# Eight PSUM-to-SBUF adds of one batch moved from VectorE to ScalarE copies and GpSimd adds, and one scalar load moved behind the first keys

## The chip, the cores and the metric

The kernel runs on one core of one Trainium2 chip. The time is the device time of one execution, in microseconds (us); times are compared as medians of several executions. The engines are named as in the profile: PE (TensorE; PEld is its weight load), DVE (VectorE), ACT (ScalarE), POOL (GpSimd) and SP (SyncE, which only issues transfers here). Each engine works through its own instructions in the order in which the program lists them.

## The reference: what is computed

Thresholded attention, then one block of an MLP mixer, all in float32. Batch 8, 8 heads, 576 tokens, 64 columns per head, so 512 columns per token.

```
scores = q @ k.T / 8
scores = where(scores >= max(scores) - tau, scores, -1e9)
attn   = exp(scores - max(scores)); attn /= sum(attn) + 1e-9
x      = (attn @ v), heads side by side         # (8, 576, 512)
h      = relu(x.T @ w_tok1) @ w_tok2            # over tokens: 576 -> 256 -> 576
u      = x + h.T
out    = u + relu(u @ w_ch1) @ w_ch2            # over columns: 512 -> 1536 -> 512
```

## The kernel before, in words

The work goes in *units* of 128 query tokens for one pair of heads: 18 units for each batch, 144 in all. Unit u runs `scores(u)` (L304 matmuls into PSUM, L309 row maximum on DVE, L310 bias on POOL), `weigh(u)` (ACT: L319 `e`, which thresholds, and L326, the exponential with its row sum), and one unit later `norm` (L333 and L334 on DVE, L337 on POOL). Two units later the weights `e` are turned: in batch 0 by PE (L355) and copies (L357), from batch 1 on by DVE's block transposes (L367) and sixteen transfers issued by SP (L376). `values` multiplies them with v (L411, L416), which leaves x, transposed, in the tile `xT` (by L423 on DVE in batch 0, L421 on ACT after that).

The MLP of one batch is a list of steps with costs, laid between the units of the next batch: `fill(share)`, called at several places of each unit, takes steps from the deque `todo` until a quota of cost is used up. `token_mlp(b)` gives the steps `turn_x` (PE transposes L447, copied to `x_sb` by ACT, L448), `tok1` (L454, relu to `a` by ACT L456) and `tok2` (L464: one product of 128 columns by 288 tokens into PSUM; L468: DVE adds it to `xT` in place). `channel_mlp` gives `ch1` (L507, relu to `g` by ACT L508) and `ch2` (L528). Batch 0 is special: its first two column blocks are started early, in `early`, and its last two when `push(0)` is called after its last unit. All eight `tok2` steps of batch 0 run in units 19 to 22, when the products have their own PSUM pool `ps_mm` with two buffers, shared with `ch1` and `ch2`. Until then and for some 30 us after, the weights still arrive: int64 words from memory are turned into float32 by a chain over SP (L178 load), ACT (L193, L195), DVE (L203, L205, L209) and POOL (L217, an add of two SBUF operands), one *piece* after the other, paced by `weight(2)` three times per unit.

At the start, tau is loaded by ACT's queue (L89), then the first queries by SP and the first keys by ACT, four transfers each (L105); DVE computes three small columns from tau (L265 to L269: `tlow`, `toff`, `ntau`) and then transposes queries and keys (L286). `toff` is read first by POOL's bias, `ntau` by ACT's exponential. Every transfer signals one of eight semaphores in turn, and a transfer that gets a semaphore already in use first waits for the earlier one to land.

The lines that matter:

```
439:    return (ps_mm or ps_tr).tile([P, DM], F32, tag="mm" if ps_mm else "tr", name=name)
467:    u = xT[:, c, o + HS * f : o + HS * f + HS]
468:    nc.vector.tensor_add(out=u, in0=u, in1=to)
474:    steps += [(0.97, lambda c=c, f=f: tok2(c, f)) for c in ps for f in range(2)]
```

Of the kernel before, what the change touches and what calls it, by code (L numbers as in the profile page):

```python
# [9 lines left out]
F32 = mybir.dt.float32  # L10
# [4 lines left out]
ALU = mybir.AluOpType  # L15
AX = mybir.AxisListType

P = 128
# [3 lines left out]
def kernel(  # L22
# [25 lines left out]
    nc = tc.nc  # L48
# [12 lines left out]
    NCC = DM // P  # L61
    NJ = DCH // P
    HS = S // 2
    NK = 2 * S // P
    GR = 2 * P
    SCALE = 1.0 / 8.0
# [3 lines left out]
    work = ctx.enter_context(tc.tile_pool(name="work", bufs=2))  # L70
# [7 lines left out]
    ps_mm = None  # L78
# [7 lines left out]
    UB = 9 * NP // 2  # L86

    tau_sb = const.tile([P, 1], F32, name="tau_sb")
    nc.scalar.dma_start(out=tau_sb, in_=bass.AP(tensor=tau.tensor, offset=0, ap=[[0, P], [1, 1]]))  # L89


    loaded = {}
# [3 lines left out]
    def load_qk(n, eng, parts=range(8)):  # L96


        b, p = pairs[n]
        if n not in loaded:  # L100
            loaded[n] = [ld.tile([P, S // 32, 32], F32, tag=tag, bufs=1, name=f"{tag}_{n}") for tag in ("lq", "lk")]
        for part in parts:
            i, which = divmod(part, 2)
            h, c = divmod(i, 2)
            eng[which].dma_start(  # L105
                out=loaded[n][which][32 * i : 32 * i + 32],
                in_=(q, k)[which][b, 2 * p + h, :, 32 * c : 32 * c + 32].rearrange("(n t) d -> t n d", t=32),
            )
# [11 lines left out]
    for t in vlast:  # L120
        nc.gpsimd.memset(t, 0.0)
    load_qk(0, (nc.sync, nc.scalar))

    w1 = const.tile([P, NT, DTOK], F32, name="w1")
    w2 = const.tile([P, NTK, S], F32, name="w2")
# [117 lines left out]
    def need(i):  # L243

        weight(3 * i + 4 - steps_done)
# [14 lines left out]
    FAR = 104.0  # L260
    STEEP = 3.0e38
    tlow = const.tile([P, 1], F32, name="tlow")
    toff = const.tile([P, 1], F32, name="toff")
    ntau = const.tile([P, 1], F32, name="ntau")
    nc.vector.tensor_scalar(out=tlow, in0=tau_sb, scalar1=0.0, scalar2=-3.0e38, op0=ALU.is_lt, op1=ALU.mult)  # L265
    nc.vector.tensor_scalar(out=toff, in0=tau_sb, scalar1=0.0, scalar2=FAR, op0=ALU.max, op1=ALU.min)
    nc.vector.tensor_scalar(out=toff, in0=toff, scalar1=-1.0 / SCALE, scalar2=None, op0=ALU.mult)
    nc.vector.tensor_add(out=toff, in0=toff, in1=tlow)
    nc.vector.tensor_scalar(out=ntau, in0=toff, scalar1=SCALE, scalar2=None, op0=ALU.mult)  # L269


    heads = {}
# [8 lines left out]
    def prep(n):  # L281
        lq, lk = loaded.pop(n)
        made = []
        for src, name in ((lq, "qT"), (lk, "kT")):
            sb = work.tile([P, S], F32, tag=name, name=f"{name}_{n}")
            nc.vector.transpose(out=sb, in_=src.rearrange("p n d -> p (n d)"))  # L286
            made.append(sb)
        heads[n] = made
# [135 lines left out]


    hidden = {}

    def token_mlp(b, ps=range(NP)):

        xT = xTs[b]  # L430
        o = S * (b % 2)
        L = len(ps)
        cols = slice(P * ps[0], P * ps[0] + P * L)
        if b not in hidden:
            hidden[b] = work.tile([P, NTK, DM], F32, tag="a", bufs=1, name=f"a_{b}")
        a = hidden[b]

        def psum(name):
            return (ps_mm or ps_tr).tile([P, DM], F32, tag="mm" if ps_mm else "tr", name=name)

        def turn_x(t, n):
            M = MT[t]
            to = ps_tr.tile([P, MAIN], F32, tag="tr", name=f"tx_{b}_{t}_{ps[0]}")[0:M, 0 : n * L * P].rearrange("p (t c x) -> p t c x", t=n, c=L)
            for i in range(n):
                for c in range(L):
                    tok = o + (t + i) * P
                    nc.tensor.transpose(out=to[:, i, c, :], in_=xT[:, ps[c], tok : tok + M], identity=ident)  # L447
            nc.scalar.copy(out=x_sb[0:M, t : t + n, cols], in_=to.rearrange("q t p d -> q t (p d)"))  # L448

        def tok1(m):  # L450
            need(2)
            to = psum(f"t1_{b}_{m}_{ps[0]}")[:, 0 : P * L]
            for t in range(NT):
                nc.tensor.matmul(to, lhsT=w1[:, t, P * m : P * m + P], rhs=x_sb[:, t, cols], start=(t == 0), stop=(t == NT - 1))  # L454
            if ps_mm:
                nc.scalar.activation(out=a[:, m, cols], in_=to, func=AF.Relu)  # L456
            else:
                copies.append(lambda: nc.vector.tensor_scalar(out=a[:, m, cols], in0=to, scalar1=0.0, scalar2=None, op0=ALU.max))

        def tok2(c, f):  # L460
            need(6)
            to = psum(f"t2_{b}_{c}_{f}")[:, 0:HS]
            for m in range(NTK):
                nc.tensor.matmul(  # L464
                    to, lhsT=a[:, m, P * c : P * c + P], rhs=w2[:, m, HS * f : HS * f + HS], start=(m == 0), stop=(m == NTK - 1)
                )
            u = xT[:, c, o + HS * f : o + HS * f + HS]
            nc.vector.tensor_add(out=u, in0=u, in1=to)  # L468

        n = NI // L  # L470
        steps = [(0.11 * n * L, lambda t=t: turn_x(t, n)) for t in range(0, NI, n)] + [(0.11 * L, lambda: turn_x(NI, 1))]
        first = len(steps)
        steps += [(1.1 * L, lambda m=m: tok1(m)) for m in range(NTK)]
        steps += [(0.97, lambda c=c, f=f: tok2(c, f)) for c in ps for f in range(2)]
        return steps, (first, first + NTK)


# [101 lines left out]
    def push(b):  # L579
        nonlocal quota  # L580
        uT = xTs[b]
        steps, waits = token_mlp(b) if b else token_mlp(b, range(NP // 2, NP))
        old = list(todo)
        todo.clear()
        todo.extend(early)
        early.clear()

        for i, step in enumerate(steps):
            n = 2 if i in waits else 1
            todo.extend(old[:n] + [step])  # L590
            del old[:n]
        todo.extend(old)
        for i in range(2) if b % 2 == 0 else range(2, (2 * S + GR - 1) // GR):
            todo.extend(channel_mlp(b - b % 2, uT, i))
        quota = (sum(c for c, _ in todo) - (KEEP if b else KEEP_FIRST)) / (UB - 1)

    prep(0)
    due = deque()
    b_now = 0
    LAG = 2  # L600
# [13 lines left out]
    for u in range(len(units) + LAG + 4):  # L614
        on = u < len(units)
        if u == UB:
            late.close()
            ps_mm = ctx.enter_context(tc.tile_pool(name="ps_mm", bufs=2, space=bass.MemoryType.PSUM))
        if on:
            b_now, p0, t = units[u]  # L620
            n = b_now * NP + p0
# [24 lines left out]
        if last and u < UB:  # L646
            early.extend(token_mlp(0, range(NP // 2))[0])
        elif last:
            push(0)
# [79 lines left out]
```

## Time and profile before

| | us |
|---|---|
| median of 5 executions | 1358.22 |
| lowest, highest | 1352.83, 1359.95 |
| the profiled execution | 1359.95 |
| its span, first to last instruction | 1358.2 |
| busy in the span: PE | 1311.8 (97%) |
| DVE | 593.3 (44%) |
| ACT | 585.9 (43%) |
| POOL | 355.5 (26%) |
| mean granted PE clock | 0.992 |
| the eight adds of L468 in batch 0 | 441 to 455 ns each, from 112.5 to 144.7 us |

A profile is one execution seen by the hardware profiler. Its span is cut into 40 equal slices, with the busy share of each engine as a digit (tenths, 9 is 90% or more) and the clock that PE was granted. The *chain of waits* is followed back from the last instruction: at each step to what released it. Groups and timelines name an instruction by line, engine and operation, then `output<-inputs`; in square brackets stands how long the engine was idle before it, and what ended that. Two engines that meet in a tile wait for each other through semaphores.

### The profile page before, as it was taken

How to read it: one execution, taken by the hardware profiler on the slowest of the kernel's cores; microseconds unless marked ns; L12 is line 12 of the kernel's file. 1: busy time of each engine (PE TensorE's matmuls, PEld its weight loads, DVE VectorE, ACT ScalarE, POOL GpSimd, SP SyncE). 2: the span in 40 equal slices, each digit the busy share in tenths (PEclk: the TensorE clock that was granted, in tenths of full speed). 3: DMA queues.
4: the chain of work that ended last, by engine and by line, in shares of the span. 5: the costliest groups of instructions: out<-in, count | busy, mean ns of one | idle time of the engine just before them, and what ended most of it. 6: DMA issues, size and time to landing. Idle time of an engine off the chain costs nothing.

```text
span 1358.2 us, 17794 instructions
## 1 busy us (share of the span) xinstructions
PE 1311.8 (97%) x6138; PEld 811.6 (60%) x6138; DVE 593.3 (44%) x1024; ACT 585.9 (43%) x1299; POOL 355.5 (26%) x683
## 2 busy tenths in 40 slices
PE   6888899999999999999999999999999999999998
PEld 4555655547575566565656566465656476575675
DVE  5888874435443444534344444435443454201000
ACT  5776654445454444443435444344434453120110
POOL 4665653223222222212122222212221222100000
PEclk9998899999999999999999999999999999999999
DMA  5434764545454444443445435534443453400000
GB/s 122 105 92 126 203 154 102 122 104 118 100 125 100 95 112 109 116 109 86 96 99 125 104 77 119 135 81 106 115 103 82 111 120 76 112 24 17 23 24 32
DMA packets 296538, 135.31 MB, mean 100 GB/s; under 512 B 204736, under 2 KB 289216, under 8 KB 296448
## 3 DMA queue, kind: packets, MB, share of 16 engines
q1 hardware_dynamic: 167840, 118.15, 34.2%
q10 hardware_dynamic: 128608, 16.01, 7.4%
q8 instruction: 49, 0.80, 0.3%
q14 instruction: 41, 0.34, 0.1%
HBM read 43.25 MB, written 9.44 MB: 39 GB/s over the span
## 4 chain that ended last, share of the span: by engine, by line
PE 85%; DVE 6%; DMA 3%; ACT 3%; issue 1%; POOL 1%; SPq 0%; ACTq 0%; DVEq 0%; POOLq 0%
PE c L528 27%; PE c L507 26%; PE sc L304 11%; PE pv L416 9%; PE t L454 5%; PE t L464 4%; PE pv L411 3%; DVE mx L309 2%; ACT e L319 1%; PE tr L355 1%; PE tx L447 1%; DMA lq<-in_q_dram 1%; DMA lk<-in_k_dram 1%; ACT e L326 1%; DVE wc L205 1%
## 5 line engine op out<-in xcount | busy, mean ns | idle before, releaser
L309 DVE TENSOR_REDUCE mx<-sc 128x1 f32<-128x576 f32 x288 | 204.3, 750 | 451.8 <-PE sc L304 451.7
L507 PE MATMUL c<-xT,wc 128*128 128x256 f32 (+1 forms) x1920 | 401.3, 363 | 0.2 <-ACT g L508 0.2
L528 PE MATMUL c<-wc,g 128*128 128x512 f32 x864 | 389.5, 597 | 0.0
L507 PEld LDWEIGHTS c<-xT,wc 128*128 128x128 f32 x1920 | 335.0, 191 | 70.2 <-issue 30.1
L310 POOL TENSOR_SCALAR bias<-mx,toff 128x1 f32<-128x1 f32 x288 | 83.2, 289 | 781.8 <-DVE mx L309 725.4
L319 ACT ACTIVATE e<-sc,bias 128x576 f32<-128x576 f32 x288 | 199.6, 740 | 179.7 <-POOL bias L310 175.5
L528 PEld LDWEIGHTS c<-wc,g 128*128 128x128 f32 x864 | 158.9, 190 | 181.6 <-issue 178.2
L326 ACT ACTIVATE e<-e,ntau 128x576 f32<-128x576 f32 x288 | 221.0, 771 | 0.0
L337 POOL TENSOR_SCALAR e<-e,rr 128x576 f32<-128x576 f32 x288 | 215.1, 759 | 14.0 <-ACT g L508 2.6
L508 ACT ACTIVATE g<-c 128x256 f32<-128x256 f32 (+1 forms) x240 | 86.9, 362 | 297.2 <-PE c L507 279.1
L304 PE MATMUL sc<-kT,qT 64*128 64x288 f32 (+1 forms) x1280 | 195.5, 440 | 12.3 <-DVE kT L286 7.3
L367 DVE STREAM_TRANSPOSE T<-e 128x1152 f32<-128x1152 f32 x126 | 172.0, 1365 | 5.5 <-DMA eT<-T 3.3
L304 PEld LDWEIGHTS sc<-kT,qT 64*128 64x128 f32 (+1 forms) x1280 | 107.4, 181 | 100.6 <-issue 57.3
L416 PE MATMUL pv<-eT,lv 128*64 128x384 f32 (+1 forms) x1024 | 138.3, 411 | 0.0
L416 PEld LDWEIGHTS pv<-eT,lv 128*64 128x64 f32 x1024 | 77.0, 139 | 50.0 <-issue 41.3
L421 ACT COPY xT<-pv 128x384 f32<-128x384 f32 (+1 forms) x56 | 21.0, 400 | 167.8 <-PE pv L416 161.8
L540 DVE TENSOR_TENSOR us<-c,ut 128x512 f32<-128x512 f32 x27 | 18.6, 691 | 155.0 <-PE c L528 142.1
L464 PE MATMUL t<-w,a 128*128 128x288 f32 x256 | 76.0, 424 | 8.1 <-DVE xT L468 4.7
L454 PE MATMUL t<-x_sb,w 128*128 128x512 f32 (+1 forms) x180 | 72.6, 550 | 0.0
L464 PEld LDWEIGHTS t<-w,a 128*128 128x128 f32 x256 | 46.1, 193 | 30.3 <-issue 10.5
L468 DVE TENSOR_TENSOR xT<-xT,t 128x288 f32<-128x288 f32 x64 | 28.3, 446 | 71.0 <-PE t L464 70.5
L326 ACT ACTIVATION_READ_ACCUMULATOR e<-e,ntau 128x1 f32 x288 | 56.5, 196 | 0.0
(46 smaller groups left out, 545.7 us busy)
## 6 DMA issues: line engine op xcount, KB each, us to landing
eT<-T SPq DMA_DIRECT2D x672, 108.0 KB, 2.3
scratch<-in_moe_w_ch_dram SPq DMA_DIRECT2D x24, 512.0 KB, 3.6
lv<-in_v_dram SPq DMA_DIRECT2D x32, 288.0 KB, 3.3
out_dram<-us SPq DMA_DIRECT2D x36, 256.0 KB, 2.2
lk<-in_k_dram ACTq DMA_DIRECT2D x111, 72.0 KB, 2.8
lq<-in_q_dram ACTq DMA_DIRECT2D x106, 72.0 KB, 2.3
ut<-us SPq DMA_DIRECT2D x192, 32.0 KB, 1.9
lq<-in_q_dram SPq DMA_DIRECT2D x22, 72.0 KB, 3.2
```

The lines of the kernel that those rows point to most:

```text
L304: nc.tensor.matmul(sc[h][rows, f, 0:HS], lhsT=qT[r, cols], rhs=kT[r, HS * f : HS * f + HS], start=True, stop=True)
L309: nc.vector.tensor_reduce(out=mx[:, c], in_=sc[h][:, :, 0:HS], axis=AX.XY, op=ALU.max)
L319: nc.scalar.activation(out=eh, in_=sc[h][:, :, 0:HS], func=AF.Prelu, bias=bias[:, h : h + 1], scale=SCALE, alpha=STEEP)
L326: nc.scalar.activation(out=eh, in_=eh, func=AF.Exp, bias=ntau, accum_out=rs[:, h : h + 1])
L337: nc.gpsimd.tensor_scalar(out=eh, in0=eh, scalar1=rr[:, h : h + 1], scalar2=1.0, op0=ALU.mult, op1=ALU.mult)
L367: nc.vector.transpose(out=T[:, :, place, :].rearrange("p a (c x) -> p c a x", c=NK), in_=e.rearrange("p (c a x) -> p c a x", c=NK, a=4))
L416: nc.tensor.matmul(to[r], lhsT=lv[:, j, :], rhs=e[j], start=False, stop=(c == NI - 1), skip_group_check=True)
L454: nc.tensor.matmul(to, lhsT=w1[:, t, P * m : P * m + P], rhs=x_sb[:, t, cols], start=(t == 0), stop=(t == NT - 1))
L464: nc.tensor.matmul(to, lhsT=a[:, m, P * c : P * c + P], rhs=w2[:, m, HS * f : HS * f + HS], start=(m == 0), stop=(m == NTK - 1))
L507: nc.tensor.matmul(ps, lhsT=wc1[:, j, c, :], rhs=uT[:, c, GR * i : GR * i + n], start=(c == 0), stop=(c == NCC - 1))
L508: nc.scalar.activation(out=s["g"][:, j, 0:n], in_=ps, func=AF.Relu)
L528: nc.tensor.matmul(flat, lhsT=s["g"][:, j, P * t : P * t + P], rhs=wc2[:, j, :], start=(j == 0 and b > 0), stop=(j == NJ - 1), skip_group_ ...
```

## The change

- The eight `tok2` products of batch 0 are no longer added to `xT` by DVE from PSUM. ACT copies the product to one third of a scratch tile `h` in SBUF (the thirds are used in turn; `h` lies in the buffer `ut`, which is first needed with batch 2), and POOL adds `h` to `xT`. All other batches keep DVE's add.
- For batch 0, the `tok2` steps run all first halves of the tokens, then all second halves, instead of both halves of one column block after the other.
- The five operations on tau are the same as before, moved. The load of tau stands behind the four key transfers on ACT's queue instead of ahead of them, and DVE's five operations on tau stand behind the transposes of the first queries and keys. Tau's transfer now takes the semaphore of the first key transfer, and waits for that one; the fourth key transfer no longer waits for tau.

```diff
     tau_sb = const.tile([P, 1], F32, name="tau_sb")
-    nc.scalar.dma_start(out=tau_sb, in_=bass.AP(tensor=tau.tensor, offset=0, ap=[[0, P], [1, 1]]))
...
     load_qk(0, (nc.sync, nc.scalar))
+    nc.scalar.dma_start(out=tau_sb, in_=bass.AP(tensor=tau.tensor, offset=0, ap=[[0, P], [1, 1]]))
...
+    stage = []
+    turns = [0]
...
             u = xT[:, c, o + HS * f : o + HS * f + HS]
-            nc.vector.tensor_add(out=u, in0=u, in1=to)
+            if b == 0 and ps_mm:
+                h = work.tile([P, GR // P, 4, NCC * 32], F32, tag="ut", bufs=1, name=f"h_{c}_{f}") if not stage else stage[0]
+                if not stage:
+                    stage.append(h)
+                h = h.rearrange("q n a x -> q (n a x)")[:, HS * (turns[0] % 3) : HS * (turns[0] % 3) + HS]
+                turns[0] += 1
+                nc.scalar.copy(out=h, in_=to)
+                nc.gpsimd.tensor_tensor(out=u, in0=u, in1=h, op=ALU.add)
+            else:
+                nc.vector.tensor_add(out=u, in0=u, in1=to)
...
-        steps += [(0.97, lambda c=c, f=f: tok2(c, f)) for c in ps for f in range(2)]
+        order = [(c, f) for c in ps for f in range(2)]
+        if b == 0:
+            order.sort(key=lambda x: x[1])
+        steps += [(0.97, lambda c=c, f=f: tok2(c, f)) for c, f in order]
...
     prep(0)
+    nc.vector.tensor_scalar(out=tlow, in0=tau_sb, scalar1=0.0, scalar2=-3.0e38, op0=ALU.is_lt, op1=ALU.mult)
+    nc.vector.tensor_scalar(out=toff, in0=tau_sb, scalar1=0.0, scalar2=FAR, op0=ALU.max, op1=ALU.min)
+    nc.vector.tensor_scalar(out=toff, in0=toff, scalar1=-1.0 / SCALE, scalar2=None, op0=ALU.mult)
+    nc.vector.tensor_add(out=toff, in0=toff, in1=tlow)
+    nc.vector.tensor_scalar(out=ntau, in0=toff, scalar1=SCALE, scalar2=None, op0=ALU.mult)
```

More of the change, by code (lines that the diff above doesn't have):

```diff
@@ L264 @@
     ntau = const.tile([P, 1], F32, name="ntau")
[L265 to L269, printed above, removed]
     heads = {}
```

## The prediction

> **What bounds the kernel now.** I read the slices over the span first, then the busy time by stage, then the chain of work inside the stage that the change touches.
>
> ```profile
> PE   6888899999999999999999999999999999999998
> DVE  5888874435443444534344444435443454201000
> PEclk9998899999999999999999999999999999999999
> ```
>
> TensorE (PE) is full from the sixth slice (34 us each) to the end; VectorE (DVE) is nearly full in slices two to five only, and there alone the clock row falls to 8. By stage (core time of the stage, then PE, PEld, DVE, ACT, POOL busy, clock):
>
> ```profile
> 100.00:180.00 80.00, 71.62 (x319) 47.34 (x317) 68.77 (x113) 53.85 (x112) 48.84 (x58) 0.89 0.60 160
> 300.00:600.00 300.00, 296.44 (x1464) 183.73 (x1464) 135.09 (x228) 137.02 (x309) 77.88 (x166) 1.00 0.46 106
> ```
>
> From 300 us on PE idles 3.6 us in 300, and the change leaves PE's later work as it is. A gain or loss is thus a shift of the moment, near 180 us, at which PE becomes the bound; all of the change but the tau load lies before it. The eight adds of L468 that change run from 112.5 to 144.7 us. The chain of waits there, merged (start, us, what):
>
> ```profile
> 124.90 0.04 DVE xT L468
> 124.94 0.34 issue
> 125.28 1.37 DVE T L367
> ...
> 138.91 1.33 DVE mx L309 x2
> ...
> 141.23 0.45 DVE xT L468
> 141.69 0.04 issue
> 141.73 2.29 PE t L464 x4
> 144.02 3.41 PE c L507 x8
> 147.43 1.49 PE sc L304 x8
> ```
>
> The chain is VectorE's own order nearly throughout; the adds stand in it, and the last second product (L464) waits 2.9 us for an add to free its PSUM buffer.
>
> **The eight adds leave VectorE.** Each took 441 to 455 ns, 8 x 0.446 = 3.6 us off VectorE. Not all of that was on the path. One add (136.66) sat where L205 behind it had to wait for a GpSimd add anyway, and two (123.93, 124.90) where VectorE waited for PE; without them the transpose at 125.28 can go 2.2 us earlier, after the L423 copy (ends 123.34).
>
> **ScalarE gets eight copies.** Nearest rows: L508, PSUM 128x256, 362 ns; L421, 128x384, 400 ns. I take 0.39, 3.1 us in all, on an engine busy 54 of 80 us. The length is not the cost; the place is. In the built order of the changed kernel, the copies of the second and third product stand on ScalarE ahead of L195 and of both e of L319, and the matmuls that they wait for end late:
>
> ```profile
> 122.66 3.18 PE L464 MATMUL t<-w,a 128*128 128x288 f32 x12
> ```
> ```profile
> 121.79 0.70 ACT L195 ACTIVATE scratch<-scratch 128x512 f32<-128x512 f32 x1 [1.33 <-DVE wc L205]
> 122.40 1.34 ACT L319 ACTIVATE e<-sc,bias 128x576 f32<-128x576 f32 x2
> ...
> 126.31 1.07 ACT L448 COPY x_sb<-tx 128x512 f32<-128x512 f32 x2 [1.81 <-PE tx L447]
> ```
>
> The three products end near 123.8, 124.8 and 125.8. The first two copies end at 124.1 and 125.1, so L195 starts at 125.1, not 121.79: 3.3 us late. ScalarE has 1.8 us of idle time ahead of L448, and a third copy (0.39) comes in between, so the copies to x_sb come 3.3 - 1.8 + 0.4 = 1.9 us late. PE then waits for x_sb with nothing else in its order, and the scores behind (129.45) slide with it. VectorE reaches its next reduction (130.99) about when it did, but its scores aren't there: they were ready some 0.5 us before. The stage is 1.9 - 0.5 = 1.4 us late, 1.4 + 1.7 = 3.1 if PE's clock then halves for one stretch of 3.4 us (below). I take 2.0.
>
> **GpSimd gets eight adds.** Its row for two SBUF operands of that size:
>
> ```profile
> L217 POOL TENSOR_TENSOR w<-w,scratch x2: 807/832/857, 61.3 to 65.0; 128x288 int32<-128x288 int32 x2
> ```
>
> That is integer; in f32 the lower end is half of L337's 735 ns for 576 columns, 0.37. I take 0.8: 6.4 us in 80, of which GpSimd is busy 49. Again the place counts. Beside GpSimd's L217, VectorE's L203 and L205 stretch, and end only after it:
>
> ```profile
> 134.66 3.24 POOL L217 TENSOR_TENSOR wc<-wc,scratch 128x512 int32<-128x512 int32 x2
> ```
> ```profile
> 135.22 1.52 DVE L203 TENSOR_SCALAR scratch<-scratch 128x512 f32<-128x512 f32 x1
> 136.66 0.44 DVE L468 TENSOR_TENSOR xT<-xT,t 128x288 f32<-128x288 f32 x1
> 137.03 1.15 DVE L205 TENSOR_SCALAR wc<-scratch 128x512 uint32<-128x512 uint32 x1
> ```
>
> L203 takes 0.41 alone and L205 0.44. L468 in between is not stretched. So an add that VectorE did freely becomes one that can hold up VectorE's neighbours: each costs between -0.45 (no neighbour meets it) and +0.8 (one waits it out). Here the fifth add comes right behind these two L217, where L209 would run; I put 0.6 on the path for it, and nothing for the other seven, where one engine or the other waits for PE, ScalarE or a transfer anyway. If that cover is gone, two more at 0.6 add 1.2. The Trainium skill (SBUF — State Buffer, section "SBUF: two separate sides") says that VectorE and GpSimd lock a shared port pair for a whole instruction, and that a VectorE operation with two SBUF inputs counts too; the old add has one input in PSUM. By that rule alone, with every add met, the change would cost up to 8 x 0.83 - 3.6 = 3.1 us; the row at 137.03 agrees that there is such a wait.
>
> **The stall at 141.73.** It does not go. The copy that now frees this buffer stands on ScalarE behind L193, which waits for a weight transfer until 139.76; 139.76 + 0.65 + 0.35 = 140.8 against 141.73, 1.0 us earlier at most, less the 2.0 from above. And the first L507 now needs the GpSimd add of the sixth product, behind the two L383 copies that end at 144.85: 145.6 at the earliest, when before the whole of L507's first group had run by 147.43. So the wait changes its name, and there is no gain here.
>
> What follows hangs on GpSimd too: the transfers of eT are issued from 144.23, behind a weight transfer that waits for the L217 ending at 143.82, and at 155.25 the chain is the next weight transfer (3.96 us) behind them. All of that shifts by 2.0 + 0.6 = 2.6 us, and with it the stretch to 180.
>
> **Other order, tau.** First tokens first moves four products and no work. The sharing of one h tile in three parts: each copy waits for an add three back, long done. At the start, tau's transfer (0.73 to 3.62) held up the fourth key transfer, which the chain shows next (3.62, 2.84 us); now the keys go at once. But VectorE transposes the queries first, at 5.64 for 0.78, and the keys' transpose began at 6.49: 0.14 us is all that the keys can win, unless the queries land earlier or later for sharing with them (between -0.3 and +0.3). Tau now waits for the first key transfer: the first query transfer had landed by 3.79, so by about 3.8, plus 2.9, tau lands near 6.7; its five small operations (3.63 to 4.41, 0.8 us) then fit before the first reduction at 9.64, while VectorE waits 2.38 us for the scores. ScalarE's table load (1.28) slides from 3.98 to 4.3, needed at 10.89. Should tau land after 8.8, the excess is paid in full. I take -0.1.
>
> **Sum.** 2.0 + 0.6 - 0.1 = +2.5 us. The profiled execution took 1359.95 (span 1358.2 and 1.75 around it): 1362.4. It is 1.7 us above the median shown, 1358.22, so as a median 1360.7. A measurement of this kernel tells about 0.3%, 4.1 us, from no change: this forecast lies inside.
>
> **Rivals.**
> - *The adds were the path* (faster, 0.12). For it: the chain names L468 and the 2.9 us wait. If ScalarE's copies delay nothing, the 3.6 us come back, 0.1 at the start, and half of one 3.4 us stretch of slow clock (1.7): -5.4, 1352.8. Against: the products end after ScalarE wants to go on.
> - *PE falls to half clock* (slower, 0.28). After a stretch of 3.4 us in which PE is busy only 1.12 us (137.69 to 141.10), the clock is 0.50 for two stretches, to 147.9; after 1.91 us busy it is 0.50 for one. 2.84 us cost nothing. The new wait for x_sb leaves PE idle some 2 us around 127 to 130. If PE is busy there for less than about 2.3 us of a stretch and loses two stretches, 3.4 us are added to the 1.9 of the copies, with the 0.6 of the lock: +5.9, 1364.1. The skill's page on TensorE (TensorE: Matmul & The Clock Gate, "What's actually happening") asks for a whole idle window of 3.4 us before the clock halves; by it this rival would cost nothing beyond the wait. The rows above differ: half a window was enough.
> - *Nothing shows* (0.60 together with the forecast): ScalarE's delay is eaten by waits for transfers around 155, and the shift is 0 to 2.5.
>
> Chances: faster by over 0.3% 0.10, within 0.58, slower 0.32 (the half clock, and the upper part of the forecast). The range goes from 1355.0 (part of the gain, no delay) to 1366.0 (half clock and two more locked adds, 5.9 + 1.2, rounded up).
>
> **What would show it.** Right: ScalarE idle 1 us and more ahead of the new copies near 123 to 125, L195 and e of L319 behind them late; x_sb late and PE waiting for it; L203, L205 or L209 stretched beside the new GpSimd adds; a wait of PE for GpSimd at the first L507; and keys' transpose near 6.35 with the tau operations done before 9.6. Wrong: L448 no later than before, counted from the scores ahead of it; no stretch of half clock near 141 to 148; or a first reduction later than 9.7 because tau is late.

## The result, and the profile after

The changed kernel took 1357.40 us (median of 36 executions, 1354.28 to 1361.55). The kernel before, run between them, took 1356.29 us (62 executions, 1352.77 to 1360.03). The ratio is 1.0012, with a 95% interval of 1.0006 to 1.0017: by the ratio the change costs 1.6 us (0.8 to 2.3); the two medians differ by 1.1 us. It is a small loss, too small for a single execution to tell. The predicted 1360.7 is 3.3 us above the measured median. The forecast loss was 2.5 us, and the kernel before came out 1.9 us under the median that the prediction started from (1356.29 against 1358.22).

The profiled execution of the changed kernel took 1356.88 us, with a span of 1355.0 us. That is 3.2 us *shorter* than the span of the profile of before, although the kernel is slower. One profile against another tells nothing here about the whole; what can be compared are the lengths of the steps inside. In the changed kernel the lines have other numbers: the scores are L299 (before: L304), the row maximum L304 (L309), `e` L314 (L319), the copy to `x_sb` L445 (L448), `tok2` L461 (L464), `ch1` L517 (L507). The new copy is L472, the new add L473.

The slices over the span, the same three rows:

```profile
PE   6887899999999999999999999999999999999998
DVE  6888874535443444534344444434443454201000
PEclk9998999999999999999999999999999999999999
```

The two stages (core time, PE, PEld, DVE, ACT, POOL busy, clock):

```profile
100.00:180.00 80.00, 66.19 (x302) 43.82 (x303) 68.49 (x104) 53.64 (x113) 55.40 (x65) 0.94 0.60 158
300.00:600.00 300.00, 295.88 (x1462) 183.88 (x1457) 135.04 (x228) 137.38 (x310) 77.87 (x166) 1.00 0.46 107
```

From 300 us on nothing has changed. In the stage of the change, GpSimd has 6.6 us more to do (48.84 before). VectorE has 9 instructions fewer, yet its busy time is only 0.3 us less (68.77 before). The two windows don't hold quite the same work, but much of what left VectorE came back in longer instructions, as will be seen. The chain of waits of the same stage:

```profile
122.65 0.40 ACT h L472
...
123.63 1.26 ACT e L314 x2
124.90 0.29 ACT h L472
...
125.95 0.48 ACT x_sb L445
...
126.48 0.41 PE tx L444 x2
...
129.05 1.22 PE sc L299 x8
130.27 1.40 DVE mx L304 x2
...
142.35 1.75 POOL wc L217
144.10 0.39 POOL vl L378
...
145.03 1.21 POOL xT L473
...
146.28 1.22 PE c L517 x2
147.50 2.27 PE sc L299 x8
```

The reader is to see two new pieces. From 122.65 to 126.44 the chain is ScalarE's: copy, L195, `e`, copy, exponential, then `x_sb`. Before, this stretch was VectorE's own order. From 142.35 to 146.23 it is GpSimd's: a weight add, the two copies to `vl`, and the new add, for which the first `ch1` products wait; the scores behind them then take 2.27 us (1.49 before), because PE's clock is at half from 146.16 to 149.57 us. ScalarE's order in the first of these stretches, with the idle time before each in brackets:

```profile
121.68 0.40 ACT L472 COPY h<-t 128x288 f32<-128x288 f32 x1 [3.92 <-PE t L461]
...
125.83 1.09 ACT L445 COPY x_sb<-tx 128x512 f32<-128x512 f32 x2
```

ScalarE stands idle for 3.92 us with L195 and `e` behind the copy, and L445 has no idle time ahead of it: before, it waited there for PE (1.81), now PE waits for it. PE's waits in this profile:

```profile
PE c L517 <- POOL xT L473: 3.7, 1, 3.7
...
PE tx L444 <- ACT x_sb L445: 2.0, 1, 2.0
```

VectorE and GpSimd next to each other, at the fifth add; first VectorE, then GpSimd:

```profile
137.53 1.17 DVE L209 SCALAR_TENSOR_TENSOR wc<-scratch,wc 128x512 uint32<-128x512 uint32 x1
```
```profile
137.17 0.98 POOL L473 TENSOR_TENSOR xT<-xT,h 128x288 f32<-128x288 f32 x1
```

L209 lasts 1.17 us, with the add beside it until 138.15 us, and ends 0.55 us after the add. At the same place in e12, without such an add, it lasts 0.69 us.

**Step lengths.** The cleanest measure in a profile is the time from the start of the row maximum of one unit to that of the next: it holds little of what happened earlier. From all 14 profiles (us):

| kernel | 19 to 20 | 20 to 21 | 21 to 22 | 22 to 23 | sum | 23 to 27 |
|---|---|---|---|---|---|---|
| before, first profile | 8.10 | 11.72 | 7.84 | 10.07 | 37.73 | 33.57 |
| before, again (e12) | 8.30 | 12.13 | 7.84 | 10.04 | 38.30 | 33.27 |
| tau alone (e1) | 8.30 | 11.93 | 7.83 | 9.94 | 37.99 | 33.54 |
| order alone (e2) | 8.28 | 12.21 | 7.84 | 10.07 | 38.40 | 33.25 |
| tau and order (e7) | 8.29 | 12.02 | 7.83 | 9.99 | 38.13 | 33.26 |
| changed, first profile | 8.64 | 13.67 | 8.36 | 11.13 | 41.81 | 33.26 |
| changed, again (e9) | 8.65 | 12.49 | 8.36 | 11.13 | 40.63 | 31.97 |
| without tau (e3) | 8.64 | 12.50 | 8.36 | 11.14 | 40.63 | 32.05 |
| ACT copies, DVE adds (e4) | 8.40 | 14.76 | 8.25 | 8.90 | 40.30 | 35.24 |
| DVE copies, POOL adds (e5) | 8.65 | 13.72 | 8.31 | 10.02 | 40.69 | 33.28 |
| late copies (e6) | 8.65 | 12.21 | 8.36 | 10.51 | 39.73 | 33.24 |
| first four only (e11) | 8.64 | 13.20 | 7.87 | 9.21 | 38.92 | 33.54 |
| second PSUM pool (e8) | 8.09 | 11.71 | 7.83 | 8.31 | 35.94 | 35.28 |
| second PSUM pool, again (e10) | 8.31 | 12.06 | 7.84 | 8.31 | 36.51 | 33.97 |

The five kernels that keep VectorE's adds in the old PSUM pool need 38.1 us for these four steps on average; the three that make all eight copies and adds in the new way need 41.0. Of these 2.9 us, 0.9 come back by unit 27 (33.4 against 32.4 us), and 2.0 us stay. The medians of e3, which has everything but tau's move, differ from before by 2.0 too (its ratio says 1.6, between 0.1 and 3.0).

The first, third and fourth step are steady within 0.25 us for kernels alike. The second step is not, and it comes apart when it is cut at the start of the second, third and fourth product on PE. First the kernel before (e12), then the changed one (e9):

```profile
121.43 3.18 PE L464 MATMUL t<-w,a 128*128 128x288 f32 x12
...
128.22 1.24 PE L304 MATMUL sc<-kT,qT 64*128 64x288 f32 x8
```
```profile
119.56 3.18 PE L461 MATMUL t<-w,a 128*128 128x288 f32 x12
...
128.13 1.24 PE L299 MATMUL sc<-kT,qT 64*128 64x288 f32 x8
```

From the products to the scores it is 6.79 us in the one (128.22 - 121.43) and 8.57 in the other. It is 6.79 or 6.78 in all seven kernels with VectorE's adds from PSUM, and in e5; 8.57 or 8.58 in the five with the ScalarE copies in the old place (both profiles of the changed kernel, e3, e4, e11); 7.40 in e6. From the products to the row maximum of unit 21 it is 8.33 and 9.84: the copies cost 1.5 us here, in every profile. What scatters is the piece ahead, from the row maximum of unit 20 to the products: 3.4 to 3.9 us in the seven, 2.6 to 4.9 in the others, as a stretch of PE's half clock lies over more or less of it (until 118.9 us in the first profile of the changed kernel, with 3.8 us; until 116.9 in e9, with 2.6).

Two pairs of profiles show what is left when the slow stretches lie alike, counted from the row maximum of unit 19 to the products. In e11 and e12 the stretch ends 9.97 and 10.00 us after that row maximum, and the products come after 12.00 and 12.10 us. In e3 and e8 it ends after 8.83 and 8.76 us, and the products come after 11.29 and 11.48. So the 0.4 us by which the first step is longer with the new adds (8.64 to 8.65) is gone by the time of the products: VectorE's row maximum is late, PE is not, and the piece ahead of the products is shorter for it.

### The profile page after: what moved, and what is told of

It reads as the page before. It is cut to its first block, busy times and chain, and to the rows that moved or that the text cites. A ratio compares the mean times of both kernels' runs of the same rounds, so it can differ in the third digit from the quotient of the medians.

```text
span 1355.0 us, 17799 instructions
## 1 busy us (share of the span) xinstructions
PE 1304.7 (96%) x6138; PEld 807.3 (60%) x6138; DVE 594.1 (44%) x1016; ACT 588.0 (43%) x1307; POOL 363.2 (27%) x691
## 4 chain that ended last, share of the span: by engine, by line
PE 86%; DVE 6%; ACT 3%; DMA 2%; POOL 1%; issue 1%; SPq 0%; ACTq 0%; DVEq 0%; POOLq 0%
PE c L538 27%; PE c L517 26%; PE sc L299 11%; PE pv L411 8%; PE t L451 5%; PE t L461 4%; PE pv L406 3%; DVE mx L304 2%; ACT e L314 1%; PE tx L444 1%; DMA lk<-in_k_dram 1%; DMA lq<-in_q_dram 1%; PE tr L350 1%; DVE scratch L203 1%; ACT e L321 1%
## 5 line engine op out<-in xcount | busy, mean ns | idle before, releaser
L517 PE MATMUL c<-xT,wc 128*128 128x256 f32 (+1 forms) x1920 | 400.3, 362 | 4.0 <-POOL xT L473 3.7
L304 DVE TENSOR_REDUCE mx<-sc 128x1 f32<-128x576 f32 x288 | 204.3, 750 | 450.8 <-PE sc L299 450.8
L517 PEld LDWEIGHTS c<-xT,wc 128*128 128x128 f32 x1920 | 333.9, 190 | 74.1 <-issue 28.9
L314 ACT ACTIVATE e<-sc,bias 128x576 f32<-128x576 f32 x288 | 199.6, 740 | 180.1 <-POOL bias L305 177.0
L299 PE MATMUL sc<-kT,qT 64*128 64x288 f32 (+1 forms) x1280 | 194.6, 437 | 11.1 <-DVE kT L281 7.3
L299 PEld LDWEIGHTS sc<-kT,qT 64*128 64x128 f32 (+1 forms) x1280 | 107.9, 180 | 98.1 <-issue 57.3
L461 PE MATMUL t<-w,a 128*128 128x288 f32 x256 | 74.1, 416 | 7.0 <-ACT g L518 3.2
L461 PEld LDWEIGHTS t<-w,a 128*128 128x128 f32 x256 | 45.4, 190 | 28.9 <-issue 10.5
L475 DVE TENSOR_TENSOR xT<-xT,t 128x288 f32<-128x288 f32 x56 | 24.8, 447 | 69.5 <-PE t L461 69.0
```

Source lines behind the costliest of these rows:

```text
L299: nc.tensor.matmul(sc[h][rows, f, 0:HS], lhsT=qT[r, cols], rhs=kT[r, HS * f : HS * f + HS], start=True, stop=True)
L304: nc.vector.tensor_reduce(out=mx[:, c], in_=sc[h][:, :, 0:HS], axis=AX.XY, op=ALU.max)
L314: nc.scalar.activation(out=eh, in_=sc[h][:, :, 0:HS], func=AF.Prelu, bias=bias[:, h : h + 1], scale=SCALE, alpha=STEEP)
L461: nc.tensor.matmul(to, lhsT=a[:, m, P * c : P * c + P], rhs=w2[:, m, HS * f : HS * f + HS], start=(m == 0), stop=(m == NTK - 1))
L517: nc.tensor.matmul(ps, lhsT=wc1[:, j, c, :], rhs=uT[:, c, GR * i : GR * i + n], start=(c == 0), stop=(c == NCC - 1))
```

## The experiments

Each kernel ran twelve times, beside the kernel before. e1 to e4 were run together (before: 1357.94 us), e5 to e8 together (before: 1354.05), e9 to e12 together (before: 1354.43), each of these the median of 35 executions. The three groups ran on three chips, so times are compared within a group only. The ratio is not the quotient of the two medians, and with so few executions the two can differ by more than the effect: where they do, both are given.

**e1, tau alone.** The kernel before with tau's load and its five operations moved as in the change, and nothing else:

```diff
-    nc.scalar.dma_start(out=tau_sb, in_=bass.AP(tensor=tau.tensor, offset=0, ap=[[0, P], [1, 1]]))
...
     load_qk(0, (nc.sync, nc.scalar))
+    nc.scalar.dma_start(out=tau_sb, in_=bass.AP(tensor=tau.tensor, offset=0, ap=[[0, P], [1, 1]]))
...
     prep(0)
+    nc.vector.tensor_scalar(out=tlow, in0=tau_sb, scalar1=0.0, scalar2=-3.0e38, op0=ALU.is_lt, op1=ALU.mult)
...
```

> Before, with the load of tau and its five small operations moved alone; all adds stay on VectorE. Theory (the small loss of 1.6 us is what is left of a local loss of some 4 us in units 20 to 23, and the start changes nothing): the keys' transpose still follows the queries', first reduction at 9.6 as in both profiles, time within 0.5 us of before. Rival (the start gives back 2 us that hide most of the loss): 1.5 to 2.5 us faster than before, ratio 0.9982 to 0.9989.

Measured: 1357.00 us, ratio 0.9993 (0.9982 to 1.0004). The first row maximum, which ends the start, began at 9.61 us; with tau loaded first it began at 9.64, 11.04, 10.37 and 10.03 us in the four profiles of such kernels (before, e2, e3, e12), 10.27 on average. In the ten profiles with tau moved it began between 9.43 and 9.77, 9.61 on average. So the move gains some 0.7 us at the start, and mostly takes away a scatter. The chain of waits of the kernel before, in its second profile (e12), shows where it came from:

```profile
0.73 2.87 DMA tau_sb<-in_tau_dram
...
3.62 3.23 DMA lk<-in_k_dram
...
6.88 0.79 DVE kT L286
```

Tau's 512 bytes take 2.87 us, the fourth key transfer waits for them, and then takes 3.23 us. In the profile that the prediction read it had taken 2.84 us: just short enough for the keys to be there when VectorE was done with the queries.

**e2, the order alone.** The kernel before with the sort of the `tok2` steps.

```diff
-        steps += [(0.97, lambda c=c, f=f: tok2(c, f)) for c in ps for f in range(2)]
+        order = [(c, f) for c in ps for f in range(2)]
+        if b == 0:
+            order.sort(key=lambda x: x[1])
+        steps += [(0.97, lambda c=c, f=f: tok2(c, f)) for c, f in order]
```

> Before, with only the order of the eight products changed: first tokens first, adds still on VectorE. Theory: no work moves and VectorE's adds stand at the same places, so within 0.5 us of before. Rival (the order is what costs, since the buffers of the products come free in another order): 1 us or more slower, with the wait of TensorE for VectorE's add (2.9 us before) longer or twice.

Measured: 1357.37 us, ratio 0.9989 (0.9978 to 1.0000). Its four steps take 38.40 us against 37.73 and 38.30 for the kernel before: the order costs nothing that shows, and a small gain can't be told from none.

**e3, everything but tau.** The changed kernel with tau's load and operations where they were (the diff of e1 the other way round).

> The changed kernel with tau as before: ScalarE copies, GpSimd adds, first tokens first. Theory: as the changed kernel, 1.6 us over before (1.0 to 2.2), with the waits for x_sb near 124 to 126 and for the GpSimd add at the first product of the channel MLP. Rival (tau hides 2 us of loss): 3 to 4 us over before.

Measured: 1359.90 us, ratio 1.0012 (1.0001 to 1.0022). With e1 and e2 not slower than before, the loss is in the copies and adds.

**e4, ScalarE copies, VectorE adds.** The changed kernel, with one line other:

```diff
-                nc.gpsimd.tensor_tensor(out=u, in0=u, in1=h, op=ALU.add)
+                nc.vector.tensor_tensor(out=u, in0=u, in1=h, op=ALU.add)
```

> The changed kernel, with the add of the SBUF tile on VectorE instead of GpSimd; ScalarE's copies, the order and tau as changed. It takes away GpSimd's part. Theory (ScalarE's copies cost about 2 us in unit 20, GpSimd's adds 0.5 in each of units 20 and 22 and 1 at the first product of the channel MLP): the shift from unit 20 to 21 stays near +2, the other two fall below 0.5, in all 0 to 1 us over before, better than the changed kernel by 1 to 2. Rival (the copies cost little, GpSimd's adds all of it): 1 us or more faster than before, no shift in unit 20.

Measured: 1358.18 us, ratio 1.0007 (0.9995 to 1.0018). PE's wait for `x_sb` is there in full (2.0 us), the wait of `ch1` for GpSimd is gone, and the last step falls to 8.90. The second step is long for another reason: the slow stretch lasts until 121.7 us, and 4.91 us lie ahead of the products. By the ratio the whole is 1.0 us above before (between -0.7 and 2.4), which can be told neither from no loss nor from that of the change. The add on VectorE is not what it was, however:

```profile
128.14 1.54 DVE L473 TENSOR_TENSOR xT<-xT,h 128x288 f32<-128x288 f32 x1
```

With one operand in PSUM it took 0.44 us beside GpSimd's L217. With both in SBUF it takes 1.54 us here, and 0.46 where GpSimd has nothing to do. That is the rule which the prediction took from the Trainium skill (SBUF — State Buffer, "SBUF: two separate sides"): a VectorE operation with two SBUF inputs is shut out by a GpSimd operation that reads SBUF. Here a run shows it, and it makes the copy to SBUF the step that exposes the add.

**e5, VectorE copies, GpSimd adds.**

```diff
-                nc.scalar.copy(out=h, in_=to)
+                nc.vector.tensor_copy(out=h, in_=to)
```

> The changed kernel, with the product copied out of PSUM by VectorE (288 columns, near 0.45 us, where the add stood) and added by GpSimd; tau and order as changed. ScalarE has no copies, so what is left is GpSimd's part. Theory: the reduction of unit 21 shifts by less than 0.7 us against unit 20 (it was 1.95 with ScalarE's copies), units 19 to 20 and 21 to 22 each lose about 0.5, the wait for the GpSimd add at the first channel product stays above 2 us; in all 0 to 2 us over before. Rival (GpSimd's adds alone make the whole loss): as slow as the changed kernel or slower, with unit 21 late by 2 again.

Measured: 1356.18 us against 1354.05, ratio 1.0013 (1.0002 to 1.0024): as slow as the change. PE's wait for `x_sb` falls to 0.2 us, so it was L472 on ScalarE that made the copies to `x_sb` late. But the third step is as long as in the change (8.31), and the first (8.65). VectorE does the copy in the 0.46 us of the old add, and loses again beside GpSimd's new adds. The 13.72 of the second step is not ScalarE's: in this profile PE ran at half clock from 114.4 to 121.2 us, VectorE waited 2.54 us for `values`, and the piece ahead of the products is 4.90 us. Behind the products the scores come on time (6.79), but the row maximum comes 0.5 us late (8.81 against 8.33), as VectorE's last L209 stretched to 1.17. The expectation, a shift under 0.7 us, holds for that part alone.

**e6, late copies.** In the changed kernel, the second and third product leave PSUM behind `e` of the unit instead of ahead of it:

```diff
-                nc.scalar.copy(out=h, in_=to)
-                nc.gpsimd.tensor_tensor(out=u, in0=u, in1=h, op=ALU.add)
+                def leave():
+                    nc.scalar.copy(out=h, in_=to)
+                    nc.gpsimd.tensor_tensor(out=u, in0=u, in1=h, op=ALU.add)
+
+                if (c, f) in ((1, 0), (0, 1)):
+                    late_copies.append(leave)
+                else:
+                    leave()
...
+        while late_copies:
+            late_copies.popleft()()
```

The last two lines stand in `weigh`, behind the loop over `e`.

> The changed kernel, with ScalarE's copies of the second and third product standing behind the two thresholding operations of that unit instead of ahead of them; nothing else moves. Theory (the place of the copies costs, not their length): L195 and e are on time again, the copies to x_sb are late by at most 0.8 us instead of 1.9, the shift from unit 20 to 21 falls from 1.95 to 0.5 to 1.0, and the time falls by 1 to 1.5 us against the changed kernel, to within 0.7 of before. Rival (eight copies cost by their 3.1 us of ScalarE time wherever they stand): the shift stays at 2.

Measured: 1355.68 us, ratio 1.0009 (0.9999 to 1.0019). PE's wait for `x_sb` falls from 2.0 to 0.9 us. So the place of these two copies on ScalarE made that step long. From the products to the scores it is 7.40 us, 0.6 more than with the old adds instead of 1.8. The whole stays 1.6 us above before by the medians and 1.2 by the ratio, with an interval that reaches 1, so the expected 0.7 us or less is not shown. The wait for GpSimd (3.7 us) is still there.

**e7, tau and order, old adds.** The changed kernel with VectorE's add from PSUM:

```diff
-            if b == 0 and ps_mm:
...
-                nc.scalar.copy(out=h, in_=to)
-                nc.gpsimd.tensor_tensor(out=u, in0=u, in1=h, op=ALU.add)
-            else:
-                nc.vector.tensor_add(out=u, in0=u, in1=to)
+            nc.vector.tensor_add(out=u, in0=u, in1=to)
```

> Before, with tau moved and the eight products in the new order, adds on VectorE: the change without ScalarE and GpSimd. Theory: the first reduction at 9.6 to 9.8 us (9.64 to 11.04 in the three profiles with tau first), so 0.5 to 1 us faster than before on average, and no shift over 0.5 us in units 19 to 23. Rival (what tau gains is luck of one execution): same as before within 0.3.

Measured: 1355.00 us, ratio 0.9997 (0.9985 to 1.0008). Without the copies and the new adds every step is as in the kernel before (e12) within 0.2 us. By the ratio the loss is gone (0.4 us under before); by the medians it is 0.95 above, so the times alone don't settle it. The 0.5 to 1 us that tau was expected to gain does not show in the time.

**e8, the second PSUM pool.** e7, with the products of the last column block put into the other PSUM pool, so that the 2.9 us wait for a PSUM buffer has no cause:

```diff
-            to = psum(f"t2_{b}_{c}_{f}")[:, 0:HS]
+            if b == 0 and c == 3:
+                to = ps_tr.tile([P, DM], F32, tag="tr", name=f"t2_{b}_{c}_{f}")[:, 0:HS]
+            else:
+                to = psum(f"t2_{b}_{c}_{f}")[:, 0:HS]
```

> As e7, with the two products of the last column block in the other PSUM pool (ps_tr, idle in unit 22), so that the last product need not wait for VectorE's add. Theory: the 2.9 us wait of TensorE and most of the half clock behind it (6.8 us) go, the reduction of unit 23 comes 1 to 1.8 us earlier against unit 22 than before; but the weight transfer near 155 waits for GpSimd's L217 as before, so at most 0.5 us of it are left at unit 25, and the time is that of e7 or up to 0.5 us less. Rival (that wait is on the path to the end): 2 us or more under e7.

Measured: 1353.75 us, ratio 0.9990 (0.9979 to 1.0001). The wait is gone and the last step takes 8.31 us instead of 10.0. But the stretch to unit 27 takes 35.28 us instead of the 33.3 of e7, so next to nothing of it is left there in this profile, in which PE is at half clock from 161.5 to 164.9 us.

**e9, the changed kernel again.**

> The changed kernel once more, beside the three others. Theory (places of the copies and of the adds): +1.6 us over before (ratio 1.0006 to 1.0017 as measured first); TensorE waits about 2 us for x_sb near 126 and over 3 us for the GpSimd add at the first L517, in this execution too, wherever the slow-clock stretches fall. Rival (the first profile's waits were an accident of the clock's phase): one of the two waits is missing or under 1 us.

Measured: 1356.72 us, ratio 1.0015 (1.0004 to 1.0026). Both waits are there, at the same places and with the same lengths as in the first profile (2.0 us for `x_sb`, 3.7 for GpSimd), though the slow stretches of the clock fall elsewhere. Three of the four steps agree with the first profile within 0.01 us; the second is 12.49 instead of 13.67, all of it ahead of the products.

**e10, the second PSUM pool again.** The kernel of e8.

> The same kernel as e8 (tau and order moved, the products of the last column block through the other PSUM pool, VectorE's adds kept). If its gain is real: again below before, by 0.3 to 1.5 us, and 1.9 to 3 us below the changed kernel on the same chip. If e8 was chance: within 0.3 us of before.

Measured: 1353.40 us, ratio 0.9993 (0.9983 to 1.0003); 3.3 us under e9 beside it. It is clearly faster than the changed kernel. Faster than before it is twice by a little (0.3 and 1.0 us), each time with an interval that just takes in 1, so that is likely and not shown. Of the 1.7 us by which the last step is shorter, 0.7 are lost again by unit 27 (33.97 against the 33.3 of e7).

**e11, the first four only.** In the changed kernel, only column blocks 0 and 1 go over ScalarE and GpSimd:

```diff
-            if b == 0 and ps_mm:
+            if b == 0 and c < 2 and ps_mm:
```

> Only the first four second products (column blocks 0 and 1) go over ScalarE and GpSimd; the last four are added by VectorE as before. Theory (two separate places): the wait for x_sb of about 2 us stays, the wait of the first L517 for GpSimd (3.5 to 3.7 us) is gone, the loss from unit 22 to unit 23 falls from +1.06 to about 0 and the whole comes to about +0.6 us over before. Rival (the loss is all in the early copies): +1.6 as in the changed kernel. Rival (it is all in the last four): at or below before, as with tau and order alone (-0.4 or so).

Measured: 1355.47 us, ratio 1.0003 (0.9991 to 1.0015). PE's wait for `x_sb` stays (2.0 us), the wait for GpSimd at `ch1` is gone, and the third and fourth step are 7.87 and 9.21. So the two waits are separate, each with its own four products. How the loss divides between them the times can't tell: by the medians 1.0 of the 2.3 us of e9 are left, by the ratio 0.4 of 2.0, and the interval of e11 runs from -1.2 to 2.0 us. By the steps, the last four adds carry the 0.5 of the third step and, with the wait for GpSimd and the clock behind it, 1.9 of the fourth.

**e12, the kernel before as a control.**

> The kernel before, unchanged, treated as if it were a change: a control. Ratio 1.000; how far it strays from 1 is how far the other ratios can be trusted. Theory on tau: the keys' transpose begins late again, between 6.5 and 7.9 us, and the first reduction between 9.6 and 11.0, since the fourth key transfer waits for tau. Rival (the first profile was typical): 6.5 and 9.6. Theory on the clock: the slow stretches fall on another phase than in the first profile.

Measured: 1354.67 us, ratio 1.0004 (0.9990 to 1.0019). A kernel against itself strays by 0.04%, with an interval from -1.4 to 2.6 us, and two of its twelve executions took 1360.5 and 1360.6. So a difference of 0.5 us in this study says nothing, and one of 1 us between two kernels with twelve executions little. The start was as expected with tau first: the keys' transpose began at 6.88 us, the first row maximum at 10.03.

## Why the prediction was right or wrong

The forecast of a small loss, not told from no change in one execution, was right, and so were its main places. Of its terms, two were right, two were mis-sized, and two were missed.

- **Eight adds off VectorE give nothing back: right.** What VectorE saved it now waits. Its waits from 100 to 160 us for the scores, first in the kernel before (e12) and then in the changed one:

```profile
DVE mx L309 <- PE sc L304: 3.4, 2, 1.7
```
```profile
DVE mx L304 <- PE sc L299: 6.7, 3, 4.2
```

  3.3 us more, close to the 3.6 us of the adds: 1.8 ahead of unit 21, behind ScalarE's copies, and 2.5 ahead of unit 23 (4.2 against 1.7), behind GpSimd's add, less 1.0 ahead of unit 18, where the change has not begun. So the rival "the adds were the path" falls: they stood in the chain, but the scores came no earlier without them. Up to the products, where neither of these waits lies, the gain is 0.1 to 0.2 us in the two pairs above.
- **The place of ScalarE's copies: right in mechanism, the size too high.** Copies of 0.40 us (0.39 predicted) made PE wait 2.0 us for `x_sb` (0.2 in e12; 1.9 more was predicted). From the products on, the step 20 to 21 grew by 1.5 us, where 2.0 were put on it: 1.4 without a slow stretch of the clock, and none came. e6 moved two of the copies, and two thirds of the lateness of the scores went; e5 took ScalarE out, and all of it went.
- **The locked fifth add: right, 0.52 us for the 0.6 put on it** (step 21 to 22, 8.36 against 7.84). The seven others were put at nothing; one of them, near 110 us, lengthens L205 and, by moving L217, L209, and makes that step 0.4 longer (8.65 against 8.25 on average), but the products behind it are not late, so nothing was right for it too. The add itself takes 0.79 to 1.20 us in the first profile, with a median of 0.89, above the 0.83 that the prediction had as its upper value, from the integer row; the lower end that it took from L337 (741 ns at least in the profile, not 735) was never seen.
- **The stall that "does not go": right that it changes its name, wrong that it costs nothing.** The add ended at 146.23 (145.6 was the earliest by the prediction), and the first `ch1` group ended 8.81 us after the row maximum ahead of it (8.52 before): 0.3 us. The rest was not in the forecast: in that wait of 3.7 us PE fell to half clock, and the scores of unit 23, next in PE's order, took 2.27 us instead of 1.49. Together the step grew by 1.1 us, in all three profiles of the full change. Before, the slow stretch fell on the `ch1` products ahead of the scores and was over 0.5 us into the scores. The rival "PE falls to half clock" fails at its place: at 127 to 130 no profile shows a slow stretch. The prediction had set less than 2.3 us of PE work in a stretch as its condition; in e9, PE is busy for 1.49 of the 3.41 us from 123.71, with the new wait in them, and the clock stays full. And the slow stretch at 146 is no new one: the kernel before has one there too, 6.8 us long.
- **The stretch behind, to 180 us: predicted to keep the loss, it gave part back.** e9 and e3 make up 1.3 us between units 23 and 27 (32.0 against 33.4 on average), the first profile of after 0.1. In e9 and e3 the chain from 146 to 184 us is PE's own after the stall and names no weight transfer; in the first profile of after and in both of before it goes over one near 155 us that takes 3.5 to 4.3. So what the rival "nothing shows" expected, a part of the delay eaten behind unit 23, happened in two of three profiles. In e9 ScalarE waited 1.6 us there for the weight transfer, in the first profile 3.0; why the transfer was in time in e9 was not tested.
- **Tau: right in direction, 0.1 put on it where 0.7 was to be had at the first row maximum.** The step that failed read the start off one profile, in which the keys had come just in time. Tau itself lands later than forecast (8.1 instead of 6.7, 4.9 us after its issue at 3.18), yet its five operations were done before the scores came (first row maximum at 9.62), as the prediction needed. In e9 they end only 0.1 us ahead of it (9.32 and 9.43).

With the measured sizes the sum is 1.5 + 0.5 + 1.1 = 3.1 us for the four steps; by the table they are 2.9 us longer on average. Less 0.9 given back behind them (the mean of the three profiles) and 0.7 for tau that makes 1.3 to 1.5 us, if tau's gain reaches the end, which no time shows by itself. Measured were 1.6 (0.8 to 2.3) and, in e9, 2.0 (0.5 to 3.5). That the forecast of 2.5 came near is partly luck: the loss that it put at nothing (the stall, 1.1) and the gains that it missed (0.6 of tau's, 0.9 in the stretch behind) nearly cancel. The 1360.7 itself lies too high mostly because it started from a median of five executions, 1.9 us above that of 62.

What stays open is what sets the part that is given back, and where a stretch of half clock falls in an execution: no run here held everything else fixed and moved only that.

## What to carry to other kernels

An operation that is moved to an idle engine is priced by what is queued behind it there: copies of 0.4 us cost 1.5 us because ScalarE sat waiting for its product with L195 and `e` behind it. A wait goes when its cause goes, here with other PSUM buffers for two products (e8, e10: the step is 1.7 us shorter), and not by moving the work that it is named after; but the stretch behind took 0.7 to 2.0 us of that back, so a shorter step is not yet a shorter kernel. And a term read off a single profile needs a second one where two transfers race: the start scattered by 1.4 us over four profiles with tau loaded first.

## What the runs showed that was not expected

**A wait of 2.9 us in PE's order goes with half clock.** In the 11 profiles with one wait of PE of 2.9 us or more between 137 and 148 us, the clock is at half for 3.4 or 6.8 us, in a stretch that begins between 139.8 and 147.8. In the three without (e4, e8, e10: 1.9 us at most) there is none between 122 and 161 us. The same stage of e12 and of e10 (columns as above, the clock is the number behind POOL):

```profile
139.00:145.00 6.00, 4.50 (x10) 3.48 (x11) 5.93 (x12) 2.81 (x6) 5.74 (x7) 0.57 0.74 208
```
```profile
139.00:145.00 6.00, 5.08 (x23) 3.09 (x21) 5.93 (x12) 4.23 (x9) 4.39 (x6) 1.00 0.75 184
```

In e12, 10 matmuls take 4.50 us; in e10, 23 take 5.08. The waits were 2.90 to 3.71 us long. In e8 and e10, without wait and slow stretch, the last step is 1.7 us shorter (8.31 against 10.0). The Trainium skill (TensorE: Matmul & The Clock Gate, "What's actually happening") names an idle window of about 3.4 us as the condition, and a window that runs freely; the second agrees with stretches that begin at other times in every profile and last 3.4, 6.8 or 10.2 us, the first does not: no wait of e12 in this stage is longer than 2.91 us.

What fits better is how busy PE is in a window. Windows of 3.41 us were laid from the slow stretches of each profile, between 50 and 200 us, and PE's busy time in them read from its records. Of those with full clock, all 23 in which PE was busy for less than 1.45 us were followed by half clock; of the 75 between 1.45 and 2.4 us, 20 were; of the 457 busier ones, none. In e12 PE is busy for 1.18 us in the window ahead of its slow stretch at 139.81. So a wait of some 2 us can cost clock or not by where it falls in the windows. What decides between 1.45 and 2.4 us stays open.

**The executions of one kernel scatter.** Stretches of 3.4 us at half clock come and go between executions (one at 253.8 us in the first profile of before, none there in the 13 others); one can cost 1.7 us at most, half of its length. That the scatter comes from them is not shown: over the 35 executions of the kernel before in each of the three groups, the time goes only weakly with the mean granted clock (correlations of -0.16, -0.33 and -0.54). The kernel before ranges from 1351.0 to 1361.6 us over the three groups, the second PSUM pool, in two of them, from 1351.6 to 1355.8.
